# One bank for the four least loaded experts in w1's stage, capacities that fall by 16, and three buffers for w1's split pairs

## The chip, the cores and the metric

The kernel runs on one core of one Trainium2 chip. The metric is the device time of one execution in microseconds. The kernel before takes 1414.84 us as the median of three runs (1413.66 to 1415.68).

The engines that matter here are TensorE (PE, with weight loads shown apart as PEld), VectorE (DVE), ScalarE (ACT), GpSimd (POOL) and SyncE (SP), which issues most DMAs. Each engine works through its own queue in the order in which the kernel wrote it down.

## The reference

The output is a gated mix of an attention and a mixture of experts, both over the same 2048 rows of 448 numbers:

```python
x = A_x                                            # 1 x 2048 x 448
g = sigmoid((x * gate_w).sum(-1, keepdims=True))
a = attention(x, wqkv, wo)                         # 16 heads of 28, softmax over 2048 keys
logits = x @ w_gate                                # 8 experts
topk_idx = argsort(-logits)[:, :2]                 # each row goes to two of them
gates = softmax(the two logits)
for e in range(8):
    w = (gates * (topk_idx == e)).sum(-1, keepdims=True)
    b += w * (silu(x @ w1[e]) @ w2[e])             # w1: 448 x 1792, w2: 1792 x 448
out = g * a + (1 - g) * b
```

Only the rows that chose an expert are sent through it: 4096 pairs of row and expert, 512 per expert on average. The loads that this input gives, in falling order, are 561, 545, 514, 507, 501, 500, 497 and 471.

## The kernel before

**Precision.** Almost every product is made of three matmuls on a fast type: each operand is split into a high part (a rounded copy) and a low part (what the rounding lost), and high x high, high x low and low x high are added in PSUM. The splits are work for other engines. ACT makes the high parts, POOL (in the stage that matters here) the low ones.

**Stages.** First come the projections, the routing and its slot lists. Then, from 119 us to 885 us, come the eight experts (lines 868 to 992). The attention's scores and values fill the rest. Experts are handled in falling order of load, and expert number e of that order has `CAPS[e]` slots: `max(576 - 12*e, 512)`, so 576, 564, 552, 540, 528, 516, 512, 512. A row that finds no slot would be handled at the end by a slow loop (`spilled`); with this input none is.

**One expert** is done in two halves (`hf` 0 and 1) of 7 blocks of 128 hidden units each. Each half has a w1 stage and a w2 stage.

- *w1's stage* (line 904) makes a block of hidden units for all slots. A PSUM bank holds 512 columns, so the slots are cut into two chunks of `HC = CAPS[e] // 2` columns (288 down to 256), and each chunk takes 11 matmuls into one of two accumulators that alternate. ACT applies Silu (line 908) to each chunk as it comes out, and Copy (line 911) makes the high part `hh`. After the first chunk ACT also makes the high part of the w2 block that belongs to it (`split_w2_high`, line 767). After the second it makes, in some blocks, the high part of half a pair of w1 blocks that will be needed two blocks later (`split_w1_high`, line 730). POOL then makes, for each block and in this order, the low part of that w2 block (`w2l`, line 773), the low part of the half pair of w1 where there is one (`w1l`, line 736), and the low part of the block of hidden units before it (`hl`, line 782). The last `hl` of a half follows behind its last block. `hf32`, from which `hl` is made, has three buffers.
- *w2's stage* (line 956) adds up the outputs: four tiles of 128 slots, 21 matmuls of 448 columns each. The first tile already needs, in its 18 first matmuls, the low parts of blocks 1 to 6, and in the 20th and 21st `w2l` and `hl` of the last block. In the second half the next expert's rows are turned by TensorE between these matmuls (`turn_x`, line 755, after matmuls 6 and 15 in the first tile).
- Slots over 512 form a fifth, small tile. It is done by `last_slots` under a condition `tc.If(cnt > 512)` that every engine evaluates (line 934), after the third matmul of each w2 stage, for all experts with more than 512 slots of capacity: numbers 0 to 5.

**w1's split pairs.** Each w1 pair (256 hidden units) has a high and a low tile, two buffers of each; the first pair of all lies in another tile, `wv_r`, that the first stage had left. In a half with number 0, pairs are split in blocks 3 to 6 (counted from 1), and one pair whole at the start of w2's stage. In a half with number 1, they are split in blocks 2 to 5, and two pairs whole in w2's stage.

**The stream of maxima.** The attention needs the largest score of every row, which is 1024 tiles of 128x512 scores (line 118) that DVE reduces (lines 132 and 138). These are made in the experts' stages, in between: `STEPS` lists, for each expert, half and stage, after which matmul a step of this stream falls. A step makes 6 tiles in a PSUM area of six banks; where the number is positive, it makes a seventh in the accumulator that is just free, or, if 64 tiles are complete, spends that bank on turning their maxima round (`store_max`, line 154). A negative number makes 6 tiles and touches no accumulator. Steps come until all 1024 tiles are done, and only then may the first attention scores start (`first_scores`).

Of the kernel before, what the change touches and what calls it, by code (L numbers as in the profile page):

```python
# [9 lines left out]
F32R = mybir.dt.float32r  # L10
# [3 lines left out]
ALU = mybir.AluOpType  # L14
# [7 lines left out]


STEPS = [
# [8 lines left out]
]  # L33

S, D, H, DH, E, FF = 2048, 448, 16, 28, 8, 1792
NT = S // 128
NG = H // 4
CAP = 576
# [3 lines left out]
NTL = NMAIN // 128 + NSP  # L42
NS = NMAIN + NSP * 128

CAPS = [max(CAP - 12 * p, 512) for p in range(E)]
CTS = [[128] * 4 + [c - 512] * (c > 512) for c in CAPS]
NF = FF // 128
NH = NF // 2
# [12 lines left out]
def tile_gated_mha_moe(ctx: ExitStack, tc: tile.TileContext, x, xT, wv, wqk, wo, w1, w2, out):  # L61
    nc = tc.nc
# [131 lines left out]
    def step(bank):  # L194
        if bank and flush:
            store_max(*flush.pop(0), bank)
        elif bank:
            spare.append(bank)
        next(ms, None)
        spare.clear()  # L200
# [33 lines left out]
    def first_w():  # L234
        return pe.tile([128, 4, 512], F32, name="wv_r")
# [16 lines left out]
    with ExitStack() as pa:  # L252
# [113 lines left out]
        for t in range(NT):  # L366
# [11 lines left out]
            if 7 <= t < 15:  # L378
                b, c = divmod(t - 7, 2)
# [17 lines left out]
        def tmp(name, shape, dt=F32):  # L397
            return sb.tile(shape, dt, name=name)
# [5 lines left out]
        def routing():  # L404
# [49 lines left out]
            ahead = tmp("ahead", EE)  # L454
            nc.vector.tensor_tensor(ahead, bc(key.unsqueeze(1), EE), bc(key.unsqueeze(2), EE), op=ALU.is_gt)
            yield
            pos = tmp("pos", [128, E])
            nc.vector.tensor_reduce(pos, ahead, axis=AX.X, op=ALU.add)
            yield
            cap = tmp("cap", [128, E])  # L460
            nc.vector.tensor_scalar(cap, pos, -12.0, float(CAP), op0=ALU.mult, op1=ALU.add)
            nc.vector.tensor_scalar(cap, cap, 512.0, None, op0=ALU.max)
            yield
            nc.vector.tensor_tensor(key, cnt, cap, op=ALU.subtract)
# [7 lines left out]
            for e in range(E):  # L472
                nc.vector.tensor_tensor(sbase[:, e + 1:e + 2], sbase[:, e:e + 1], nsp[:, e:e + 1], op=ALU.add)
                if e % 4 == 3:
# [13 lines left out]
                                           op0=ALU.mult, op1=ALU.add)  # L488
# [147 lines left out]
        w1rs = [load_w1(0, c) for c in range(3)]  # L636
        for i, mt in enumerate((5, 2, 6)):
# [5 lines left out]
            if i == 0:  # L643
                nc.scalar.activation(warm[:, 1:2], warm[:, 0:1], AF.Silu)
                w1p = first_w().bitcast(F32R)
                w1t = {0: (w1rs.pop(0), w1p[:, :, 0:256], w1p[:, :, 256:512])}
# [59 lines left out]
    with ExitStack() as pb:  # L706
        sb1 = pb.enter_context(tc.tile_pool(name="pb_sb1", bufs=2, reuse_waits="tile"))
# [3 lines left out]
        NP = NF // 2  # L711
# [11 lines left out]
        def split_w1_high(p, half):  # L723
            if p >= E * NP:
                return
            if p not in w1t:
                w1t[p] = (w1rs.pop(0), sb1.tile([128, 4, 256], F32R, name="w1h"),
                          sb1.tile([128, 4, 256], F32R, name="w1l"))
            r, h, l = w1t[p]
            nc.scalar.activation(h[:, :, half], r[:, :, half], AF.Copy)  # L730

# [31 lines left out]
        WHOLE, HALVES = slice(0, 256), (slice(0, 128), slice(128, 256))  # L763
# [93 lines left out]
        NM = 11  # L857

        def behind(places, i):
            if i in places:  # L860
                step(other_accumulator())
            elif -i in places:
                step(None)

        for e in range(E):
            CT, HC = CTS[e], CAPS[e] // 2
            later = CTS[e + 1] if e + 1 < E else []
            if len(CT) == 5:
                cnt = nc.values_load(cnt_i[0:1, 0, e:e + 1], min_val=0, max_val=S)
# [6 lines left out]
            for hf in range(2):  # L876
                hs = []
                lag = None
                w1_steps, w2_steps = STEPS[e][hf]
                for f in range(NH):  # L880
                    ft = hf * NH + f
                    p = e * NP + ft // 2
                    i2 = e * NF + ft

                    w2_now = [i2] if e or hf else [i2 - 1, i2][f == 0:1 + (f == NH - 1)]

                    ahead = p + 1 if 2 <= ft < 6 or ft >= 8 and ft < 12 or e == 0 and ft < 2 else None
                    w1h, w1l = w1t[p][1:]
                    fs = HALVES[ft % 2]
                    if ft == 0:  # L890
                        flush_x()
                    mms = []
                    for j in range(3):
                        mms += [(w1h[:, j, fs], xeh[:, j]), (w1h[:, j, fs], xel[:, j]),
                                (w1l[:, j, fs], xeh[:, j])]
                    mms += [(w1h[:, 3, fs], xeh[:, 3]), (w1l[:, 3, fs], xeh[:, 3])]
                    hh = sb.tile([128, 512], F32R, name="hh", bufs=8)
                    hf32 = sb.tile([128, 512], F32, name="hf32", bufs=3)
                    ht = sb.tile([128, CAP - 512], F32, name="ht", bufs=8) if len(CT) == 5 else None
                    for c in range(2):  # L900
                        cs = slice(c * HC, (c + 1) * HC)
                        pu = accumulator()
                        for i, (a, b) in enumerate(mms):
                            nc.tensor.matmul(pu[:, 0:HC], a, b[:, cs], start=i == 0, stop=i == len(mms) - 1)  # L904
                            behind(w1_steps, 2 * NM * f + c * NM + i + 1)
                        nh = min(HC, 512 - c * HC)
                        hs_ = slice(c * HC, c * HC + nh)
                        nc.scalar.activation(hf32[:, hs_], pu[:, 0:nh], AF.Silu)  # L908
                        if ht and c == 1:
                            nc.scalar.activation(ht[:, 0:CT[4]], pu[:, nh:HC], AF.Silu)  # L910
                        nc.scalar.activation(hh[:, hs_], hf32[:, hs_], AF.Copy)
                        if c == 0:
                            for i in w2_now:
                                split_w2_high(i)
                        else:
                            if ahead:
                                split_w1_high(ahead, HALVES[ft % 2])
                    for i in w2_now:
                        split_w2_low(i)
                    if ahead:  # L920
                        split_w1_low(ahead, HALVES[ft % 2])
                    if lag:
                        hidden_low(lag)
                    hl = sb.tile([128, 512], F32R, name="hl", bufs=8)
                    lag = (hh, hf32, hl)
                    hs.append((hh, hl, ht))
# [10 lines left out]
                for n_k, k in enumerate((4, 0, 1, 2, 3)):  # L937
# [13 lines left out]
                    i = 0  # L951
# [34 lines left out]
                        nc.gpsimd.tensor_tensor(yo, yo, ysb[k], op=ALU.add)  # L986
                        nc.sync.dma_start(ys_d[r0:r0 + n], yo)

                    free = {0: ((e * NP + 4, 0),), 1: ((e * NP + NP, 0), (e * NP + NP + 1, 2))}[hf]
                    for p, at in free:  # L990
                        if n_k == at:
                            split_w1_high(p, WHOLE)
# [96 lines left out]
    qs, pos, ended = {0: q}, {}, {}  # L1089
# [123 lines left out]
```

## Time and profile before

| | before |
|---|---|
| median of three runs | 1414.84 us |
| the profiled execution's own time | 1413.67 us |
| its span in the profile | 1411.9 us |
| experts' stage (first matmul of line 904 to last of line 956) | 119.2 to 884.7 us |
| steps of the stream of maxima | 118 of seven tiles, 33 of six |

The profile is one execution. A busy TensorE says little here, since matmuls are pipelined and their shown durations overlap: what counts is the time from the start of one matmul to the start of the next. The timeline shows those starts. The table of stretches gives each engine's busy time in an expert.

### The profile page before, as it was taken

Reading aid. Unit: us, or ns where it says so; the run is one execution under the profiler, and the core shown is the slowest. Engines: PE = TensorE matmul, PEld = TensorE weight load, DVE = VectorE, ACT = ScalarE, POOL = GpSimd, SP = SyncE. Lnnn points to the kernel's source line nnn. Section 1 sums busy time; section 2 is a strip of 40 time slices with the busy share of each in tenths; the row PEclk is TensorE's granted clock in tenths of the full one; section 3 lists DMA queues with packets and bytes.
Section 4 is the critical chain, followed back from the end, with each engine's and each line's share of the span. In section 5 each row is a group of like instructions: output and inputs, shape, how many; then the busy total and the mean of one; then the engine's idle time right before and its main releaser. Section 6 shows DMA issues by size and latency. Waiting matters only on the chain. (4 is left out here: it accounts for less than half of the span.)

```text
span 1411.9 us, 28709 instructions
## 1 busy us (share of the span) xinstructions
PE 1399.9 (99%) x11028; PEld 931.1 (66%) x11028; DVE 799.5 (57%) x915; ACT 912.3 (65%) x1531; POOL 641.0 (45%) x682
## 2 busy tenths in 40 slices
PE   9999999999999999999999999999999999999998
PEld 8888888878878888888788887333333333333347
DVE  5736777777878888887888887013221212211136
ACT  5335355355445544654455434999999999999981
POOL 2124587487578666875777646121121122111120
PEclk9999999999999999999999999999999999999999
DMA  9887541343233233323432221111421332141113
GB/s 337 288 279 236 168 153 58 111 130 92 87 120 117 62 118 124 98 72 109 136 124 79 74 61 40 47 51 54 126 72 44 100 85 57 45 128 46 46 39 116
DMA packets 106685, 152.81 MB, mean 108 GB/s; under 512 B 17926, under 2 KB 77523, under 8 KB 106032
## 3 DMA queue, kind: packets, MB, share of 16 engines
q1 hardware_dynamic: 97392, 129.86, 29.2%
q0 software_dynamic: 9008, 20.83, 4.8%
q8 instruction: 89, 1.46, 0.4%
q14 instruction: 52, 0.43, 0.1%
q10 hardware_dynamic: 144, 0.23, 0.1%
HBM read 115.99 MB, written 38.02 MB: 109 GB/s over the span
## 5 line engine op out<-in xcount | busy, mean ns | idle before, releaser
L138 DVE TENSOR_REDUCE mp<-pm 128x3 f32<-128x1536 f32 (+2 forms) x304 | 515.7, 1738 | 32.3 <-PE pm L118 32.3
L1103 ACT ACTIVATE P<-ps 128x1536 f32<-128x1536 f32 x254 | 367.7, 1447 | 0.0
L1112 PE MATMUL po<-P,V 128*32 128x512 f32 x2032 | 270.6, 604 | 0.0
L904 PE MATMUL acc<-xeh,w1h 128*128 128x256 f32 (+6 forms) x880 | 252.8, 296 | 0.0
L904 PE MATMUL acc<-xeh,w1l 128*128 128x256 f32 (+6 forms) x880 | 247.0, 290 | 1.1 <-POOL w1l L736 1.1
L701 PEld LDWEIGHTS ps<-Q,Kh 29*128 29x128 f32 x2032 | 77.8, 183 | 212.6 <-ACT P L1102 212.3
L773 POOL TENSOR_TENSOR w2l<-w2r,w2h 128x448 fp32r<-128x448 f32 x112 | 129.5, 1157 | 156.1 <-ACT w2h L767 113.9
L1058 POOL DMA_DIRECT2D sum_d<-osb x64 | 32.3, 518 | 369.3 <-DVE osb L1116 369.3
L904 PE MATMUL acc<-xel,w1h 128*128 128x256 f32 (+6 forms) x660 | 189.7, 287 | 0.0
L701 PE MATMUL ps<-Q,Kh 29*128 29x512 f32 x2032 | 189.2, 443 | 0.0
L904 PEld LDWEIGHTS acc<-xeh,w1h 128*128 128x128 f32 x880 | 165.8, 188 | 25.4 <-issue 25.2
L956 PE MATMUL acc<-w2h,hh 128*128 128x448 f32 x448 | 171.2, 382 | 1.2 <-PEq L787 0.3
L904 PEld LDWEIGHTS acc<-xeh,w1l 128*128 128x128 f32 x880 | 166.0, 189 | 6.0 <-issue 2.9
L956 PE MATMUL acc<-w2h,hl 128*128 128x448 f32 x448 | 166.4, 371 | 0.2 <-POOL hl L782 0.2
L956 PE MATMUL acc<-w2l,hh 128*128 128x448 f32 x448 | 166.2, 371 | 0.0
L908 ACT ACTIVATE hf<-acc 128x256 f32<-128x256 f32 (+6 forms) x224 | 86.3, 385 | 113.6 <-PE acc L904 97.4
L1116 DVE COPY osb<-po 128x512 f32<-128x512 f32 x16 | 11.1, 692 | 261.3 <-PE po L1112 212.3
L1102 ACT ACTIVATE P<-ps 128x512 f32<-128x512 f32 x254 | 151.7, 597 | 1.4 <-ACT P L1103 0.5
L736 POOL TENSOR_TENSOR w1l<-w1r,w1h 128x512 fp32r<-128x512 f32 (+1 forms) x88 | 138.4, 1572 | 24.3 <-ACT w1h L730 20.3
L132 DVE TENSOR_REDUCE mp<-acc 128x1 f32<-128x512 f32 x118 | 81.6, 692 | 117.5 <-PE acc L118 110.4
L782 POOL TENSOR_TENSOR hl<-hf,hh 128x512 fp32r<-128x512 f32 x112 | 144.3, 1296 | 0.0
L904 PEld LDWEIGHTS acc<-xel,w1h 128*128 128x128 f32 x660 | 124.6, 189 | 1.3 <-issue 1.1
(214 smaller groups left out, 1987.1 us busy)
## 6 DMA issues: line engine op xcount, KB each, us to landing
w2r<-in_w_dram SPq DMA_DIRECT2D x112, 224.0 KB
w1r<-in_w_dram SPq DMA_DIRECT2D x56, 384.0 KB
ys_d<-zero_d SPq DMA_DIRECT2D x32, 224.0 KB
qkh_d<-hi SPq DMA_DIRECT2D x28, 256.0 KB
qkl_d<-lo SPq DMA_DIRECT2D x28, 256.0 KB
w1r<-in_w_dram SPq DMA_DIRECT2D x112, 64.0 KB
ys_d<-yo SPq DMA_DIRECT2D x32, 224.0 KB
v_d<-v_s SPq DMA_DIRECT2D x16, 256.0 KB
```

Source lines behind the costliest of these rows:

```text
L132: nc.vector.tensor_reduce(mp[:, o:o + 1], banks[0], axis=AX.X, op=ALU.max)
L138: nc.vector.tensor_reduce(mp[:, (o + lo) % 256:(o + lo) % 256 + hi - lo], pm[:, lo:hi], axis=AX.X, op=ALU.max)
L701: nc.tensor.matmul(banks[j], k[rw, ks], q[rw, c], start=i == 0, stop=i == 2)
L736: nc.gpsimd.tensor_tensor(l[:, :, half], r[:, :, half], h[:, :, half].bitcast(F32), op=ALU.subtract)
L773: nc.gpsimd.tensor_tensor(w2l, w2r, w2h.bitcast(F32), op=ALU.subtract)
L782: nc.gpsimd.tensor_tensor(hl, hf32, hh[:, 0:512].bitcast(F32), op=ALU.subtract)
L904: nc.tensor.matmul(pu[:, 0:HC], a, b[:, cs], start=i == 0, stop=i == len(mms) - 1)
L908: nc.scalar.activation(hf32[:, hs_], pu[:, 0:nh], AF.Silu)
L956: nc.tensor.matmul(py[:n, 0:D], a[:, cs], b, start=i == 0, stop=i == 3 * NH - 1)
L1102: nc.scalar.activation(P[:, 0], p1, AF.Exp, scale=SCALE)
L1103: nc.scalar.activation(P[:, 1:4], p3, AF.Exp, scale=SCALE)
L1112: nc.tensor.matmul(po[32 * j:32 * j + 32], v[:, kt % 8, 32 * j:32 * j + 32], P[:, j] if n > 1 else P[j], start=kt == 0, stop=kt == NT - 1)
```

## The change

- `CAPS` falls by 16 per expert: 576, 560, 544, 528, 512, 512, 512, 512. The routing's formula is changed with it.
- An expert with 512 slots (numbers 4 to 7) takes w1's stage in one chunk of 512 columns. A block is then 11 matmuls into one bank, one Silu and one Copy; `split_w2_high` and `split_w1_high` both follow after that one chunk. Experts 4 and 5 have no fifth tile any more.
- Every third pair of w1 lies in `wv_r`, so that there are three buffers.
- With the third buffer, the sixth pair is split whole in the w2 stage of half 0, and half 1 splits w1 pairs in blocks 4 and 5 alone.
- `STEPS` has new places. They hold 155 steps: 94 of seven tiles and 61 of six.

```diff
 STEPS = [
-    (([17, 50, 83, 116, 148], [13, 32, 51, 70]), ([7, 39, 72, -100, -124, 148], [-11, -25, 39, 59, 76])),
...
-    (([17, 50, 83, 116, 149], [18, 37, 56, 75]), ([17, 50, 83, 116, -149], [-11, -25, 39, 56, 75])),
-    (([17, 50, 83, 116, 148], [15, 34, 53, 72]), ([-12, 39, 72, 105, 138], [9, 28, 47, 67])),
+    (([-24, -48, 72, -100, -124, 148], [13, 32, 51, 70]), ([7, 39, 72, -100, -124, 148], [-11, -25, 39, 59, 76])),
+    (([17, 50, 83, 116, 148], [13, 32, 51, 70]), ([7, 39, -69, 94, -123, 148], [-11, -25, 39, 59, 76])),
+    (([17, 50, 83, 116, 149], [14, 33, 52, 71]), ([-9, -35, 61, -91, 116, 148], [-11, -25, 39, 59, 76])),
+    (([17, 50, 83, 116, 148], [13, 32, 51, 70]), ([-8, -34, 60, -90, 116, 148], [-11, -25, 39, 55, 74])),
+    (([8, 28, -45, 60, -77], [16, 35, 54, 73]), ([7, -24, 39, -56, 71], [-10, -24, 38, 55, 74])),
...
+    (([8, 28, -45, 60, -77], [16, 35, 54, 73]), ([7, -24, 39, -56, 71], [12, -31, 47, 67])),
 ]
...
-CAPS = [max(CAP - 12 * p, 512) for p in range(E)]
+CAPS = [max(CAP - 16 * p, 512) for p in range(E)]
...
             if p not in w1t:
-                w1t[p] = (w1rs.pop(0), sb1.tile([128, 4, 256], F32R, name="w1h"),
-                          sb1.tile([128, 4, 256], F32R, name="w1l"))
+                if p % 3:
+                    w1t[p] = (w1rs.pop(0), sb1.tile([128, 4, 256], F32R, name="w1h"),
+                              sb1.tile([128, 4, 256], F32R, name="w1l"))
+                else:
+                    w = first_w().bitcast(F32R)
+                    w1t[p] = (w1rs.pop(0), w[:, :, 0:256], w[:, :, 256:512])
...
-            CT, HC = CTS[e], CAPS[e] // 2
+            CT = CTS[e]
+
+            HC = CAPS[e] if CAPS[e] <= 512 else CAPS[e] // 2
+            NC = CAPS[e] // HC
...
-                    ahead = p + 1 if 2 <= ft < 6 or ft >= 8 and ft < 12 or e == 0 and ft < 2 else None
+                    ahead = p + 1 if 2 <= ft < 6 or ft in (10, 11) or e == 0 and ft < 2 else None
...
-                    for c in range(2):
+                    for c in range(NC):
...
-                            behind(w1_steps, 2 * NM * f + c * NM + i + 1)
+                            behind(w1_steps, NM * (NC * f + c) + i + 1)
...
-                        else:
-                            if ahead:
-                                split_w1_high(ahead, HALVES[ft % 2])
+                        if c == NC - 1 and ahead:
+                            split_w1_high(ahead, HALVES[ft % 2])
...
-                    free = {0: ((e * NP + 4, 0),), 1: ((e * NP + NP, 0), (e * NP + NP + 1, 2))}[hf]
+                    free = {0: ((e * NP + 4, 0), (e * NP + 5, 2)), 1: ((e * NP + NP, 0), (e * NP + NP + 1, 2))}[hf]
```

More of the change, by code (lines that the diff above doesn't have):

```diff
@@ L460, in routing @@
             cap = tmp("cap", [128, E])
-            nc.vector.tensor_scalar(cap, pos, -12.0, float(CAP), op0=ALU.mult, op1=ALU.add)
+            nc.vector.tensor_scalar(cap, pos, -16.0, float(CAP), op0=ALU.mult, op1=ALU.add)
             nc.vector.tensor_scalar(cap, cap, 512.0, None, op0=ALU.max)
```

7 rows, old and new, of the table STEPS are left out of this document.

## The prediction

> **What bounds the kernel now.** I read the page's busy times first, then the stretches expert by expert, then TensorE's waits, and then the timelines of PE, ACT and POOL in the seventh expert (number 6), which already has 512 slots.
>
> ```profile
> PE 1399.9 (99%) x11028; PEld 931.1 (66%) x11028; DVE 799.5 (57%) x915; ACT 912.3 (65%) x1531; POOL 641.0 (45%) x682
> ```
>
> ```profile
> core 0: us, PE busy (x) PEld busy (x) DVE busy (x) ACT busy (x) POOL busy (x), PEclk, DMA share, GB/s
> 515.12:608.40 93.28, 92.56 (x628) 76.91 (x627) 75.53 (x64) 46.30 (x118) 65.91 (x58) 1.00 0.33 103
> 608.40:701.12 92.72, 91.73 (x624) 75.97 (x623) 75.79 (x65) 45.83 (x115) 64.60 (x55) 1.00 0.33 105
> 701.12:792.87 91.75, 91.11 (x623) 76.05 (x622) 75.07 (x63) 45.32 (x101) 64.50 (x55) 1.00 0.33 101
> 792.87:884.74 91.87, 90.48 (x624) 75.15 (x622) 70.35 (x61) 43.91 (x97) 50.23 (x41) 1.00 0.17 51
> ```
>
> ```profile
> PE acc L904 <- POOL w1l L736: 1.1, 3, 0.7
> PE acc L956 <- POOL hl L782: 0.2, 1, 0.2
> ```
>
> The stretches are experts 4, 5, 6 and 7; the waits are us in total, times and longest, from 515 to 885 us. TensorE sets the time, at full clock, and waits for little. But the few waits for POOL fall in these experts, so I look at how close POOL is. POOL in the first half of expert 6, and TensorE at the half's first matmul, w2's first, and the 22nd of w2:
>
> ```profile
> 701.12 0.28 PE L904 MATMUL acc<-xeh,w1h 128*128 128x256 f32 x1
> 711.03 1.15 POOL L773 TENSOR_TENSOR w2l<-w2r,w2h 128x448 fp32r<-128x448 f32 x1 [1.11 <-ACT w2h L767]
> 712.42 1.29 POOL L736 TENSOR_TENSOR w1l<-w1r,w1h 128x512 fp32r<-128x512 f32 x1 [0.23 <-ACT w1h L730]
> 713.66 1.30 POOL L782 TENSOR_TENSOR hl<-hf,hh 128x512 fp32r<-128x512 f32 x1
> 714.90 1.17 POOL L773 TENSOR_TENSOR w2l<-w2r,w2h 128x448 fp32r<-128x448 f32 x1
> 716.00 1.31 POOL L736 TENSOR_TENSOR w1l<-w1r,w1h 128x512 fp32r<-128x512 f32 x1
> ...
> 724.30 0.39 PE L956 MATMUL acc<-w2h,hh 128*128 128x448 f32 x1
> 726.81 2.56 POOL L782 TENSOR_TENSOR hl<-hf,hh 128x512 fp32r<-128x512 f32 x2
> 728.18 0.47 PE L956 MATMUL acc<-w2h,hl 128*128 128x448 f32 x1 [0.24 <-POOL hl L782]
> 729.95 0.38 PE L956 MATMUL acc<-w2h,hh 128*128 128x448 f32 x1
> ```
>
> From 712.42 to 729.37 POOL has no gap. It finishes 28.25 us after the half began (729.37 - 701.12), TensorE starts the 22nd matmul of w2 at 28.83, and one matmul (728.18) has already waited. So POOL's 45% hides a stretch in which it is the bound within a fraction of a microsecond. That is what the change must be weighed against.
>
> **Prices.** TensorE's starts: twelve matmuls of 512 columns later in the projections, eleven of 256, nine of 448, and one step of the stream:
>
> ```profile
> 103.16 0.39 PE L603 MATMUL pq<-xh,wqk_h 128*128 128x512 f32 x1
> 105.88 0.39 PE L603 MATMUL pq<-xl,wqk_h 128*128 128x512 f32 x1
> 797.10 0.28 PE L904 MATMUL acc<-xeh,w1h 128*128 128x256 f32 x1
> 798.42 0.28 PE L904 MATMUL acc<-xeh,w1h 128*128 128x256 f32 x1
> 822.09 0.36 PE L956 MATMUL acc<-w2h,hh 128*128 128x448 f32 x1
> 823.92 0.36 PE L956 MATMUL acc<-w2h,hh 128*128 128x448 f32 x1
> 824.88 0.47 PE L956 MATMUL acc<-w2l,hh 128*128 128x448 f32 x1
> 825.18 0.36 PE L956 MATMUL acc<-w2h,hl 128*128 128x448 f32 x1
> ```
>
> That is 2.72/12 = 0.227, 1.32/11 = 0.120 and 1.83/9 = 0.203 us from start to start, and 0.083/192 = 0.43 ns per column. The step between 823.92 and 825.18 costs 1.26 - 2 x 0.203 = 0.86.
>
> ```profile
> L908 ACT ACTIVATE hf<-acc 128x256 f32<-128x256 f32 x56 | 21.6, 385 | 27.5 <-PE acc L904 23.1 <-POOL w2l L773 3.6
> L908 ACT ACTIVATE hf<-acc 128x288 f32<-128x288 f32 x14 | 5.8, 412 | 8.6 <-PE acc L904 8.6
> L911 ACT ACTIVATE hh<-hf 128x256 fp32r<-128x256 f32 x56 | 23.4, 418 | 1.8
> L911 ACT ACTIVATE hh<-hf 128x288 fp32r<-128x288 f32 x14 | 6.2, 445 | 0.4
> ```
>
> ```profile
> 768.92 0.36 PE L956 MATMUL acc<-w2h,hh 128*128 128x448 f32 x1
> 769.12 0.39 ACT L908 ACTIVATE hf<-acc 128x256 f32<-128x256 f32 x1 [0.80 <-PE acc L904]
> 769.54 0.42 ACT L911 ACTIVATE hh<-hf 128x256 fp32r<-128x256 f32 x1
> 760.73 0.42 ACT L911 ACTIVATE hh<-hf 128x256 fp32r<-128x256 f32 x1
> 761.05 0.56 ACT L767 ACTIVATE w2h<-w2r 128x448 fp32r<-128x448 f32 x1
> ```
>
> Silu starts 0.20 after TensorE goes on, Copy 0.42 after Silu, the w2 split 0.32 after Copy and lasts 0.56. Silu and Copy grow by 27/32 = 0.84 ns per column, so by 0.22 each for 512 (estimate from these rows).
>
> **The change, part by part.**
>
> *One chunk of 512.* A block's 22 matmuls at 0.120 (2.64) become 11 at 0.227 (2.50). Alone this is 14 x 0.14 = 2.0 us for an expert with 512 slots, more for number 4, whose chunks had 264 columns. The Trainium skill's page TensorE: Matmul & The Clock Gate (section "Wait — 56ns, not 53.3ns?") says that warm matmuls follow each other after N / 2.4 GHz + 2.5 ns, which speaks against this gain: by it two of 256 would take 218.3 ns and one of 512 215.8 ns, so only 0.4 us per expert. This trace does not agree at 256, where 120 is measured against its 109.
>
> *What the one chunk delays.* The w2 split and the w1 split, which ACT made after the first and second chunk, now both come after the whole block. From the end of a block, w2h is there after 0.20 + 0.64 + 0.54 + 0.56 = 1.94 us, and POOL starts 2.03 after it. Before, w2h came after the first chunk, mostly while the second ran.
>
> *Half 0 of experts 4 to 7.* The steps fall after matmuls 8, 28, 45, 60 and 77, so the seven blocks end at 3.36, 5.85, 9.21, 11.71, 15.07, 18.42 and 20.92 us, and w2 would start at 21.78. POOL's gapless run starts with block 3's w2l at 9.21 + 2.03 = 11.24, where before it was 711.03 - 701.12 = 9.91 plus a gap of 0.23. From there five w2l at 1.11, four w1l and six hl at 1.25 (starts in the rows above) are 18.05, so POOL ends at 29.3. TensorE without waits would come to matmul 22 of w2 at 21.78 + 21 x 0.203 + 0.86 = 26.9. It waits at three places: third matmul of blocks 5, 6 and 7 for w1l (0.6, 1.1, 0.3: block 5's w1l ends at 13.6, its third matmul could start at 13.0, and so on), and for the last two hl (0.8). That makes 2.8 us of waits, and matmul 22 starts at 29.7. The same reckoning for expert 6 before gives 28.25 for POOL's end, as measured, and 28.68 for matmul 22 where the trace has 28.83, so I add 0.15: 29.85, **1.0 us later than before**.
>
> *Half 1 of these experts.* Splits in blocks 4 and 5 only. Block 4 ends at 12.57, its w2l runs to 15.7, its w1l to 16.95; block 6 wants that at 16.4 and waits 0.6; block 7's w1l ends at 20.55 and is wanted 1.1 earlier. So 1.75 us of waits, w2 starts at 23.53. With the two turns of rows (0.46 each) that then stand ahead, hl is in time in experts 4 to 6. Expert 7 turns none and waits 0.8 more. Matmul 22 starts at 29.57 against 29.20 by the same reckoning before: **0.4 later**. Where the third buffer relieves POOL (two w1l fewer here), the latency of the one-chunk block takes its place.
>
> *The condition and the fifth tile.* Experts 4 and 5 lose both. Before, expert 5:
>
> ```profile
> 676.85 0.37 PE L956 MATMUL acc<-w2h,hl 128*128 128x448 f32 x1
> 677.37 0.44 PE L956 MATMUL acc<-w2h,hh 128*128 128x448 f32 x1
> 678.53 0.66 PE L755 MATMUL acc<-ident,xg 128*128 128x128 f32 x4 [0.32 <-ACTq L934]
> ```
>
> 0.3 us at the branch and the wait of the turned rows behind it. This, the wider chunks and the fifth tile's turn are why experts 4 and 5 take 93.28 and 92.72 and expert 6 91.75. After the change the three do the same work in the same order, so all get expert 6's time plus 1.0 plus 0.4: 93.15. Expert 7 gets 91.87 + 1.2 + 0.3 = 93.4 (its own half 0 stood at 28.6). Against before: -0.1, +0.4, +1.4, +1.5, so **+3.2**.
>
> *Steps.* With 155 steps instead of 151, four more at 0.86 = **+3.4**; all four lie in experts 0 to 3 (one each). DVE does the same 1024 tiles. Places that fall closer than before in experts 0, 2 and 3 (24 to 26 matmuls between two steps of six) may wait for DVE, at most 0.2 each: +0.8 at most, of which I take 0.5.
>
> *Capacities of experts 1 to 3.* 2, 4 and 6 columns fewer per chunk, 308 matmuls each: 12 x 308 x 0.43 ns = **-1.6**. Expert 4 receives no fifth tile's rows in expert 3's second half: -0.3 (estimate: four short transposes).
>
> *Third buffer, moved split.* The sixth pair's split (one high on ACT, one low on POOL, 2.4 us) moves into half 0's w2 stage, and with it the DMA of the pair three further on, which SP issues behind it. POOL has only row fetches and another such split there, and SP's queue behind it holds loads that are wanted one half later. I cost it at nothing; without that cover it would cost its 2.4 once per expert.
>
> **Sum:** 3.2 + 3.4 + 0.5 - 1.6 - 0.3 = +5.2 us. The profiled execution's own 1413.67 gives 1418.9; it lies 1.2 below the median of the three runs, and 1414.84 + 5.2 is 1420.0. I predict 1419.6.
>
> **The rivals.**
>
> 1. *Slower through POOL's lateness* (the forecast, 0.60).
> 2. *POOL keeps up* (faster, 0.16). This is the other side: one mechanism, POOL's run in the w1 stages of experts 4 to 7. If it ended 2.8 (half 0) and 1.75 us (half 1) earlier, TensorE would wait for nothing: 4 x (2.8 + 1.75) + 0.8 = 19 us less, 1400.6. For it speaks that POOL's total in half 1 has become smaller. Against it stand the rows: POOL had no gap from 712.42 on, and its three operations take the same time whatever TensorE does. If Silu and Copy of 512 took no longer than of 256, the run would start 0.44 earlier, 8 x 0.44 = 3.5 us less, 1416.1. The sign turns where it ends 0.65 us earlier per half (5.2/8). A page's rule bears on this rival in the other direction: the Trainium skill's Perfetto Trace Analysis (section "Optimizing Scalar/DVE Operations") says that where ScalarE isn't saturated but causes bubbles elsewhere, breaking up instructions may let work finish sooner. The change does the reverse, and ACT's 45.32 us of 91.75 show that it isn't saturated.
> 3. *Gains and waits cancel* (within 0.2%, 0.13). A 512-column matmul may follow after less than 0.227 us here, since only the projections show it. The lower bound by the rows is 512 x 0.43 ns = 0.220. Then block 3 ends 33 x 0.007 = 0.23 earlier, POOL's run starts so much earlier, and 8 x 0.23 = 1.9 us fall away; without the 0.5 for DVE it is 1417.2.
> 4. *DVE becomes a second bound* (slower still, 0.11). A step of seven before:
>
> ```profile
> 748.24 0.69 DVE L132 TENSOR_REDUCE mp<-acc 128x1 f32<-128x512 f32 x1 [1.06 <-PE acc L118]
> 748.85 3.41 DVE L138 TENSOR_REDUCE mp<-pm 128x3 f32<-128x1536 f32 x2
> ```
>
> DVE needs 4.0 us for it (748.24 to 752.26). In one-chunk experts some steps follow after 15 matmuls: 15 x 0.227 + 0.86 = 4.27 us. If each of the 40 steps in those stages waited 0.15, it would be 6 us more: 1425.6. Against it: steps of seven are followed by 17 matmuls or more.
>
> **How the numbers follow.** About 0.2% (2.8 us) is what a measurement here can tell from no change. Forecast and rival 4 are slower: 0.71. Rival 3 is the same: 0.13. Rival 2 is faster: 0.16. The range from 1411.5 to 1426 takes in rivals 3 and 4 and the upper part of rival 2, and leaves out most of the rest of 2. The forecast's own range is 1417.7 to 1423.
>
> **What would show it.** TensorE's waits for w1l and hl go from 1.3 us to some 12 or more, all in experts 4 to 7. Each of these has w2's start some 23.5 to 23.8 us after the half's, in spite of fewer matmuls. POOL's last hl ends near 29.3 us in half 0. Experts 4 to 7 take about 93 us each. Silu of 512 takes about 0.6 us. There are 155 steps. Wrong it would be if POOL's run begins earlier than 11.2, or if the 512-column matmuls follow after clearly less than 0.227.

## The result, and the profile after

The changed kernel takes 1422.3 us as the median of six runs (1421.41 to 1422.84), the kernel before 1414.75 us in six runs beside it (1413.66 to 1415.68). The ratio is 1.0053, with a 95% interval from 1.0042 to 1.0064: about 7.5 us slower. The profiled execution of after took 1422.84 us (span 1421.0), 9.2 us more than that of before.

Busy times of the page, after:

```profile
PE 1399.0 (98%) x10404; PEld 889.4 (63%) x10404; DVE 798.4 (56%) x900; ACT 888.3 (63%) x1377; POOL 637.7 (45%) x668
```

TensorE issues 624 matmuls fewer and ACT 154 instructions fewer, yet the span is 9.1 us longer. The stretches, one row per expert from 0 to 7. First before, where the prediction showed only experts 4 to 7:

```profile
core 0: us, PE busy (x) PEld busy (x) DVE busy (x) ACT busy (x) POOL busy (x), PEclk, DMA share, GB/s
119.18:222.14 102.96, 101.97 (x690) 84.05 (x688) 77.15 (x64) 49.23 (x124) 70.11 (x63) 1.00 0.55 169
222.14:322.21 100.07, 100.05 (x684) 82.48 (x683) 75.70 (x65) 48.19 (x122) 68.79 (x62) 1.00 0.33 100
322.21:421.44 99.23, 99.14 (x685) 81.25 (x683) 75.54 (x64) 48.07 (x122) 68.62 (x62) 1.00 0.32 99
421.44:515.12 93.68, 92.97 (x629) 77.42 (x627) 75.50 (x64) 46.42 (x118) 66.16 (x58) 1.00 0.34 107
```

The same view of after, all eight:

```profile
119.43:223.26 103.83, 103.09 (x692) 84.50 (x691) 78.68 (x63) 49.21 (x123) 70.06 (x62) 1.00 0.55 168
223.26:324.05 100.79, 100.63 (x689) 82.56 (x688) 78.09 (x66) 48.03 (x121) 68.62 (x61) 1.00 0.33 102
324.05:424.45 100.40, 99.82 (x689) 81.09 (x687) 77.83 (x64) 47.73 (x121) 68.46 (x61) 1.00 0.30 95
424.45:519.57 95.12, 93.00 (x628) 77.04 (x627) 78.49 (x66) 45.74 (x114) 64.69 (x54) 1.00 0.35 108
519.57:613.07 93.50, 90.61 (x467) 66.19 (x465) 72.96 (x59) 40.08 (x72) 64.50 (x54) 1.00 0.32 99
613.07:706.44 93.37, 90.76 (x466) 66.33 (x465) 73.04 (x60) 40.08 (x72) 64.49 (x54) 1.00 0.33 104
706.44:799.91 93.47, 90.71 (x467) 66.30 (x466) 73.18 (x61) 40.10 (x72) 64.49 (x54) 1.00 0.31 99
799.91:893.11 93.20, 90.09 (x465) 64.92 (x463) 67.61 (x57) 38.78 (x68) 50.19 (x40) 1.00 0.16 50
```

Experts 0 to 3 take 0.87, 0.72, 1.17 and 1.44 us longer than before, 4.2 in all. Experts 4 to 7 take 0.22, 0.65, 1.72 and 1.33 us longer, 3.9 in all. In the last four rows the second number says where: 93.4 us of the stretch hold 90.7 us of busy TensorE, where before 91.75 held 91.11. The engine that sets the time now stands idle for 2.6 us and more per expert. What it waits for, in the waits of after from 119 to 893 us (total, times, longest; `wv_r` is the third buffer of the w1 pairs):

```profile
PE acc L911 <- POOL w1l L740: 5.6, 10, 0.8
PE acc L911 <- POOL wv_r L740: 3.4, 6, 0.8
PE acc L962 <- POOL hl L786: 1.6, 5, 0.4
PE acc L154 <- ACT ysb L980: 1.1, 1, 1.1
PE acc L154 <- DVE mg L147: 1.1, 4, 0.4
```

The first three rows are waits for POOL: 10.6 us against 1.3 before. The last two were not among the waits of before. The timeline of after in the first half of expert 6, which begins at 706.44:

```profile
706.44 0.39 PE L911 MATMUL acc<-xeh,wv_r 128*128 128x512 f32 x1
...
717.79 1.15 POOL L777 TENSOR_TENSOR w2l<-w2r,w2h 128x448 fp32r<-128x448 f32 x1 [1.01 <-ACT w2h L771]
718.89 1.28 POOL L740 TENSOR_TENSOR w1l<-w1r,w1h 128x512 fp32r<-128x512 f32 x1
720.23 0.50 PE L911 MATMUL acc<-xeh,w1l 128*128 128x512 f32 x1 [0.36 <-POOL w1l L740]
722.49 1.28 POOL L740 TENSOR_TENSOR w1l<-w1r,w1h 128x512 fp32r<-128x512 f32 x1
723.82 0.50 PE L911 MATMUL acc<-xeh,w1l 128*128 128x512 f32 x1 [0.75 <-POOL w1l L740]
...
728.95 1.15 POOL L777 TENSOR_TENSOR w2l<-w2r,w2h 128x448 fp32r<-128x448 f32 x1 [0.33 <-ACT w2h L771]
...
730.36 0.47 PE L962 MATMUL acc<-w2h,hh 128*128 128x448 f32 x1
733.66 2.52 POOL L786 TENSOR_TENSOR hl<-hf,hh 128x512 fp32r<-128x512 f32 x2
736.23 0.47 PE L962 MATMUL acc<-w2h,hl 128*128 128x448 f32 x1 [0.36 <-POOL hl L786]
736.54 0.36 PE L962 MATMUL acc<-w2h,hh 128*128 128x448 f32 x1
```

Here POOL's run begins 11.35 us after the half (717.79). Its only gap is one of 0.33 us (before 728.95), in which POOL itself waits for ACT's `w2h`: a block that waited for POOL ends late, and so its own split comes late to POOL. Two third matmuls and one of w2's stage wait until POOL is done, the last `hl` ends at 736.18, which is 29.74 after the half began, and the 22nd matmul of w2 follows at 30.10. Before it was 28.83.

The listed waits are smaller than the time lost. From the matmul before the wait at 720.23 to the one after it (719.37 to 720.57) it is 1.20 us. The same stretch takes 0.57 in both_early, a run described below, where no such wait stands. So a listed wait of 0.36 cost 0.63, and in the same way the one of 0.75 cost 1.01.

The rest lies in the attention. Its values matmuls, before and then after (first and last start):

```profile
L1112 PE MATMUL po<-P,V x2032: 592/593/617, 889.4 to 1370.1; 128*32 128x512 f32 x185
```

```profile
L1118 PE MATMUL po<-P,V x2032: 592/593/618, 897.8 to 1380.1; 128*32 128x512 f32 x185
```

They take 482.3 us instead of 480.7. From the last of them to the end of the span it is 40.9 instead of 41.8 us, so 0.7 us net of this execution's 9.1 belong to a stage whose code the change doesn't touch.

### The profile page after: what moved, and what is told of

Same layout as the page of the kernel before. It is cut to its first block, busy times and chain, and to the rows that moved or that the text cites. A ratio compares the mean times of both kernels' runs of the same rounds, so it can differ in the third digit from the quotient of the medians.

```text
span 1421.0 us, 27227 instructions
## 1 busy us (share of the span) xinstructions
PE 1399.0 (98%) x10404; PEld 889.4 (63%) x10404; DVE 798.4 (56%) x900; ACT 888.3 (63%) x1377; POOL 637.7 (45%) x668
## 5 line engine op out<-in xcount | busy, mean ns | idle before, releaser
L138 DVE TENSOR_REDUCE mp<-pm 128x3 f32<-128x1536 f32 (+3 forms) x312 | 529.0, 1738 | 58.9 <-PE pm L118 58.9
L915 ACT ACTIVATE hf<-acc 128x512 f32<-128x512 f32 (+8 forms) x168 | 76.6, 456 | 156.3 <-PE acc L911 150.0
L911 PE MATMUL acc<-xeh,w1l 128*128 128x512 f32 (+4 forms) x440 | 144.2, 334 | 5.6 <-POOL w1l L740 5.6
L911 PE MATMUL acc<-xeh,w1h 128*128 128x512 f32 (+4 forms) x440 | 144.2, 333 | 0.0
L132 DVE TENSOR_REDUCE mp<-acc 128x1 f32<-128x512 f32 x95 | 65.7, 692 | 97.4 <-PE acc L118 89.0
L1072 DVE RECIPROCAL rs<-rs 128x128 f32<-128x128 f32 x64 | 60.6, 946 | 104.8 <-DMA rs<-sum_d 104.8
L118 PE MATMUL pm<-khg,qg 28*128 28x512 f32 x929 | 113.4, 449 | 0.7 <-issue 0.2
L911 PE MATMUL acc<-xeh,wv_r 128*128 128x512 f32 (+4 forms) x464 | 107.1, 329 | 3.4 <-POOL wv_r L740 3.4
L911 PE MATMUL acc<-xel,w1h 128*128 128x512 f32 (+4 forms) x330 | 109.0, 330 | 0.0
L740 POOL TENSOR_TENSOR w1l<-w1r,w1h 128x512 fp32r<-128x512 f32 (+1 forms) x53 | 91.6, 1727 | 38.2 <-ACT w1h L734 17.8
```

The lines of the kernel that those rows point to most:

```text
L118: nc.tensor.matmul(banks[n], qgs[g, qt // 4][rw, (qt % 4) * 128:(qt % 4 + 1) * 128], kh[g, kc][rw], start=True, stop=True)
L138: nc.vector.tensor_reduce(mp[:, (o + lo) % 256:(o + lo) % 256 + hi - lo], pm[:, lo:hi], axis=AX.X, op=ALU.max)
L740: nc.gpsimd.tensor_tensor(l[:, :, half], r[:, :, half], h[:, :, half].bitcast(F32), op=ALU.subtract)
```

## The experiments

There are two questions. Does the lost time come from *lateness* (the splits of ACT stand behind the whole block's Silu and Copy, so POOL starts late) or from the *amount* of POOL's work in a half that got shorter? And what costs 4.2 us in experts 0 to 3, which still work in two chunks? Times are medians; the kernel before took 1413.63 us beside the first four runs and 1414.69 beside the next three. "Experts end" is the start of the last matmul of w2's stage in the profile, a cleaner measure than the whole time, since the attention adds its own variation. It is 884.4 before and 892.7 after.

| run | time | ratio to before (95%) | experts end |
|---|---|---|---|
| two_chunks | 1408.57 | 0.9962 (0.9948 to 0.9977) | 880.2 |
| w2_early | 1410.90 | 0.9979 (0.9969 to 0.9988) | 882.1 |
| both_early | 1404.07 | 0.9931 (0.9914 to 0.9948) | 875.5 |
| one_bank | 1419.84 | 1.0046 (1.0029 to 1.0062) | 891.8 |
| no_hl | 1412.58 | 0.9985 (0.9975 to 0.9994) | 882.4 |
| third_buffer | 1413.54 | 0.9995 (0.9985 to 1.0004) | 883.0 |
| late_tails | 1403.82 | 0.9921 (0.9905 to 0.9938) | 873.8 |

**Everything but the single chunk and the new steps (two_chunks).** After, with all experts in two chunks and the `STEPS` of before:

```diff
...
-            HC = CAPS[e] if CAPS[e] <= 512 else CAPS[e] // 2
+            HC = CAPS[e] // 2
...
```

> The changed kernel, but all experts keep two chunks in w1's stage and the places of the steps are those of before (151 steps). Capacities falling by 16, the third buffer and the moved split stay. Theory (the one chunk makes POOL's work late and the four steps cost 0.86 each): without both, only gains are left. Narrower chunks in experts 1 to 3 -1.6 and in 4 and 5 -1.8, the condition and the fifth tile's turns in 3 to 5 -2.9, waits for w1l in the second halves -1.4: about 1407 us. Rival (the third buffer with its moved split, or the capacities, cost the time): 1418 or more.

It took 1408.57 us, 5.1 less than before: capacities, third buffer and moved split are a gain. The stretches of its experts 0 to 3 and 4 to 7:

```profile
119.40:514.00 394.60, 392.10 (x2679) 322.68 (x2678) 303.89 (x254) 190.75 (x479) 271.31 (x238) 1.00 0.39 120
514.00:880.53 366.53, 363.42 (x2492) 303.26 (x2490) 296.79 (x250) 179.21 (x396) 243.67 (x202) 1.00 0.30 91
```

This splits the loss. From here to after, experts 4 to 7 go from 366.5 to 373.5 us: the single chunk, with the places of steps that go with it, costs 7.0 us. Experts 0 to 3 go from 394.6 to 400.1: the new steps, four of them additional, cost 5.5. Against before, the narrower chunks and the missing turn of expert 4's fifth tile bring 1.3 us in experts 0 to 3 (395.9 to 394.6). In third_buffer, below, the same experts take 395.8, so the third buffer has hardly a part in that.

**The single chunk alone (one_bank).** Before, with one chunk in experts 6 and 7, whose capacity is 512 there too, and two steps more (153) in the rows of `STEPS` of experts 0, 1, 6 and 7. Two w1 buffers, old capacities:

```diff
...
-                    for c in range(2):
+                    for c in range(NC):
...
-                        else:
-                            if ahead:
-                                split_w1_high(ahead, HALVES[ft % 2])
+                        if c == NC - 1 and ahead:
+                            split_w1_high(ahead, HALVES[ft % 2])
```

> The kernel before with one part alone: experts 6 and 7, which have 512 slots already, take w1's stage in one chunk, with the changed kernel's places of steps there (and in experts 0 and 1, so that all tiles are made: 153 steps). Two buffers, no moved split, old capacities. Theory: the first halves of 6 and 7 get 1.3 and 1.5 us longer, the second ones 1.0 and 0.5 (reckoned with four splits in blocks 2 to 5), two more steps cost 1.7: +6.1, about 1420.9 us. Rival (one chunk of 512 is a gain for TensorE, 1.2 us per expert, and the loss comes from elsewhere): 1414.

It took 1419.84 us, 6.2 more. Experts 6 and 7 take 94.4 and 94.0 us, 4.8 us more than before together, and two steps at 0.86 are 1.7. So two experts in one chunk without the third buffer cost more than 2 us each, and the last `hl` ends up to 30.5 us after its half began. Waits from 119 to 892 us:

```profile
PE acc L906 <- POOL w1l L736: 5.3, 10, 0.8
PE acc L957 <- POOL hl L782: 0.7, 2, 0.4
```

**The order of ACT's work (w2_early, both_early).** After, where ACT makes the high parts *ahead* of the block's Silu and Copy. They don't depend on the block. First only w2's:

```diff
+                    if NC == 1:
+                        for i in w2_now:
+                            split_w2_high(i)
                     for c in range(NC):
...
-                        if c == 0:
+                        if c == 0 and NC == 2:
```

> As both_early, but only the w2 block's high part is made before the block's Silu; the w1 half pair stays behind Copy. Theory: POOL's run starts earlier, but its w1l still waits for the block; waits of 1.4 us per first half and 0.6 per second are left. 9.6 us less than the changed kernel: about 1412.7 us. Rival (amount of work): 1421 to 1423.

1410.90 us, 1.8 less than reckoned. The wait for `hl` is gone, the last `hl` of first halves ends 28.3 to 28.5 us after their start, and the waits for `w1l` and `wv_r` fall from 9.0 to 3.8 us (from 119 to 884 us), where 8.0 were reckoned to be left:

```profile
PE acc L914 <- POOL w1l L740: 2.4, 5, 0.6
PE acc L914 <- POOL wv_r L740: 1.4, 3, 0.5
```

Then both splits:

```diff
+                    if NC == 1:
+                        for i in w2_now:
+                            split_w2_high(i)
+                        if ahead:
+                            split_w1_high(ahead, HALVES[ft % 2])
                     for c in range(NC):
...
-                        if c == 0:
+                        if c == 0 and NC == 2:
...
-                        if c == NC - 1 and ahead:
+                        if c == NC - 1 and NC == 2 and ahead:
```

> The changed kernel, but in one-chunk blocks ACT makes the high parts of the w2 block and of the half pair of w1 before the block's Silu, not after its Copy. No work is added or taken away on any engine. Theory (lateness of POOL's run, because its inputs come after the whole block): reckoned as in the prediction with 0.232 us per matmul, no wait is left in the halves of experts 4 to 7; matmul 22 of w2 starts 2.6 us earlier in each first half, 1.6 in three second halves and 2.4 in the last, 17.7 us in sum: about 1404.6 us. Rival (POOL's amount of work is the bound, so order on ACT helps nothing): 1421 to 1423. Rival (steps or DVE): 1419 or more.

1404.07 us, 9.6 less than before, with the same instructions as after. The experts end 17.2 us earlier than in after (892.7 to 875.5). The first half of expert 6, which begins at 698.27:

```profile
698.27 0.39 PE L916 MATMUL acc<-xeh,wv_r 128*128 128x512 f32 x1
...
704.19 0.39 PE L916 MATMUL acc<-xeh,w1h 128*128 128x512 f32 x1
...
706.20 1.15 POOL L777 TENSOR_TENSOR w2l<-w2r,w2h 128x448 fp32r<-128x448 f32 x1
...
720.32 0.47 PE L967 MATMUL acc<-w2h,hh 128*128 128x448 f32 x1
721.78 2.52 POOL L786 TENSOR_TENSOR hl<-hf,hh 128x512 fp32r<-128x512 f32 x2
725.78 0.36 PE L967 MATMUL acc<-w2h,hh 128*128 128x448 f32 x1
```

Block 3's `w2l`, with which POOL's run began at 11.35 us, now starts at 7.93 (706.20), the last `hl` ends at 26.03, and no matmul waits for POOL any more. So this half shows what TensorE alone needs: w2 starts at 22.05 and its 22nd matmul at 27.51. In after it was 23.92 and 30.10. Lateness of POOL therefore costs 2.6 us in this half. In the second halves the 22nd matmul stands at 28.33 to 28.34 in experts 4 to 6, against 30.05 to 30.11 in after. Experts 4 to 7 together:

```profile
519.99:875.89 355.90, 355.11 (x1860) 265.26 (x1858) 286.78 (x233) 159.28 (x284) 243.59 (x202) 1.00 0.30 93
```

That is 355.9 us, 17.6 less than after and 10.6 less than two_chunks, while POOL is busy for as long as in after (243.59 us against 243.67, the sum of the four rows above) and TensorE idles for 0.8 us in all. One chunk, with its places of steps, is worth 10.6 us where its splits are early, and costs 7.0 where they are late. Two chunks with early splits were not tried. In two_chunks TensorE idles for 3.1 us in these experts (366.53 less 363.42), which leaves little for earlier splits to win there.

**The amount of POOL's work (no_hl).** After, without `hl` in experts 4 to 7 (`hh` stands in its place, so the low part of the hidden units is missing from their output):

```diff
+                    if NC == 1:
+                        hs.append((hh, hh, ht))
+                        continue
...
-                hidden_low(lag)
+                if NC == 2:
+                    hidden_low(lag)
```

> The changed kernel with POOL's hl left out in experts 4 to 7: w2's stage there uses hh a second time in place of hl, so TensorE does the same number of matmuls and the low part of the hidden units is missing from these experts' output. ACT's order stays as changed. Theory (both POOL's amount of work and the lateness of its inputs): the waits for hl go, but the first w1l still comes after the block; by the prediction's reckoning waits of 1.2 us per first half and 0.6 per second are left, 10.9 us less than the changed kernel: about 1411.4 us, and waits for w1l remain in the profile. Rival (POOL's amount of work alone): no waits are left, 1404 us as with both_early. Rival (lateness alone): 1421.

1412.58 us. Seven operations of 1.25 us leave POOL's queue in each half, and TensorE still waits (from 119 to 884 us):

```profile
PE acc L911 <- POOL w1l L740: 2.9, 8, 0.4
PE acc L911 <- POOL wv_r L740: 1.5, 4, 0.4
```

So neither explanation holds alone. Taking 8.75 us of work per half from POOL lets the experts end 10.3 us earlier than in after (882.4 against 892.7); letting it begin some 3.4 us earlier, with all its work, 17.2. A delayed start and a full queue add up to the finish that TensorE waits for, and the start is the cheaper one to mend.

**The third buffer alone (third_buffer).** Before, with three buffers and the moved split:

```diff
...
-                    ahead = p + 1 if 2 <= ft < 6 or ft >= 8 and ft < 12 or e == 0 and ft < 2 else None
+                    ahead = p + 1 if 2 <= ft < 6 or ft in (10, 11) or e == 0 and ft < 2 else None
...
-                    free = {0: ((e * NP + 4, 0),), 1: ((e * NP + NP, 0), (e * NP + NP + 1, 2))}[hf]
+                    free = {0: ((e * NP + 4, 0), (e * NP + 5, 2)), 1: ((e * NP + NP, 0), (e * NP + NP + 1, 2))}[hf]
```

> The kernel before with one part alone: three buffers for w1's split pairs, the sixth pair's split moved into the first half's w2 stage. Theory (the moved split is hidden and takes two w1l off POOL in each second half): the waits for w1l in the second halves of experts 5 to 7 go, 0.3, 0.35 and 0.9 us: about 1412.3 us, 0.1% faster. Rival (the moved split stands in a queue's way, in the prediction's price up to 2.4 us per expert): slower, up to 1432.

1413.54 us, 1.2 less than before, which can't be told from no change. The waits for `w1l` of before (1.1 us) are gone, and the experts end 1.4 us earlier. The moved split costs nothing where it went.

**Expert 3's stall (late_tails).** The waits of after list one for ACT's `ysb`. TensorE in expert 3's first half, then ACT and POOL around it:

```profile
460.13 0.37 PE L962 MATMUL acc<-w2h,hl 128*128 128x448 f32 x1
461.62 0.28 PE L154 MATMUL acc<-ident,mg 128*16 128x128 f32 x1 [1.12 <-ACT ysb L980]
```

```profile
453.03 1.04 POOL L209 DMA_INDIRECT xg<-in_x_dram,idx_i  x1 [0.16 <-issue]
454.37 0.97 POOL L209 DMA_INDIRECT xg<-in_x_dram,idx_i  x1 [0.30 <-issue]
...
459.07 0.26 ACT L169 ACTIVATE xg<-xg 128x64 f32<-128x64 f32 x1 [4.93 <-issue]
460.88 0.26 ACT L169 ACTIVATE xg<-xg 128x64 f32<-128x64 f32 x1 [1.55 <-DMA xg<-in_x_dram,idx_i]
461.04 0.53 ACT L980 ACTIVATE ysb<-acc 128x448 f32<-128x448 f32 x1
```

ACT doubles the tails of the next expert's fetched rows (line 169). The first two fetches were issued at 453.03 and 454.37, ACT begins the first of them at 459.07, and the second at 460.88; the copy that empties the accumulator (`ysb`, 461.04) stands behind them. (The profile names the fetch as the cause of the second wait alone; in both_early it names it for both.) The new step after matmul 51 wants that accumulator to turn its maxima and waits 1.1 us for it. Before, ACT waited for these rows too (`ysb` at 458.13), but there the step followed after matmul 57. Both_early has the same stall, 1.7 us there, and w2_early 0.6. This run is both_early with the tails moved behind the half's last tile:

```diff
-                            for j in {0: (), 1: (0, 1)}.get(n_k, (n_k,)):
+                            for j in range(5) if n_k == 4 else ():
```

> As both_early, and ACT doubles the tails of the next expert's fetched rows (line 169) after the first half's w2 stage instead of during it. The changed kernel's profile shows a wait of 1.1 us of a step in expert 3 for ACT's ysb, and ACT waiting just before it for rows on their way. Theory: in the changed kernel the step that now stands after matmul 51 needs a bank that ACT empties only after its wait for these rows; moved behind, that wait goes (1.8 us from start to start in both_early) and 1402.2 us is left, expert 3's first half some 44.5 us instead of 46.3. Rival (that wait has another cause, or the tails are then late for the turn of rows): 1404 or more.

The stall is gone. The same step waits for nothing, and `ysb` is no longer in the list of TensorE's waits:

```profile
460.55 0.27 PE L154 MATMUL acc<-ident,mg 128*16 128x128 f32 x1
```

Expert 3's first half takes 44.61 us instead of 46.25, and the experts end 1.7 us earlier. The time, 1403.82 us, can't be told from both_early's 1404.07 and is not the 1402.2 that was expected: this execution's values matmuls took 482.8 us where both_early's took 480.8 between the first and the last. The kernel before was slower too beside this run. Against it late_tails gains 10.9 us, both_early 9.6, and the intervals of the two ratios overlap.

**The attention's variation (after_again, late_tails_again).** One more look at each of the two, unchanged, to see whether the longer values stage belongs to the program or to the execution.

> The changed kernel unaltered, one more profile. In its first profile the attention's values stage took 1.6 us longer than before from its first to its last matmul (487.4 - 5.0 against 485.8 - 5.0), in a few single passes. If that belongs to the program, it is there again at the same passes; if to the execution, it is elsewhere or gone. The experts' stage should take 773.3 us as in the first profile, to 0.3.

> late_tails unaltered, one more profile. Its attention's values stage took 2.1 us longer than both_early's, in a few single passes, which hid the 1.7 us that its experts' stage was shorter. If that belongs to the execution, the passes are elsewhere or gone, and the time of this execution is up to 2 us below 1403.8; if to the program, they are there again.

The times were 1424.01 and 1403.92 us, and the values matmuls took 482.7 and 482.1. The experts' stage of after_again took 773.3 us, as expected. Some passes of the values stage, which take 1.90 us as a rule, take 2.05 to 2.5. Numbers 67, 194 and 195 (counted from 0) were long in all four looks at these two kernels; others came and went. Before and both_early show none or one such pass.

That would speak for the program, but the other runs speak against it. Third_buffer and no_hl, two other programs, have the same three long passes. What the runs share is the chip that they ran on. The four profiles from one chip (two_chunks, w2_early, both_early, one_bank) have values stages of 480.8 to 480.9 us. The three from a second chip (no_hl, third_buffer, late_tails) have 481.8 to 483.1, the two from a third 482.7 and 482.1. The kernel before, beside them, took 1413.63, 1414.69 and 1415.33 us. On which chips the first profiles of before and after were taken is not known, and none of the other programs was profiled both on the first chip and on another. So the chip fits better than the program, but the cause stays open. It is worth 0 to 2 us of values time, of which the end of the kernel gave back 0.9 in after's first profile.

## Why the prediction was right, and where its sizes were off

The direction was as predicted, and so was the mechanism in experts 4 to 7: slower through POOL's lateness. But more than half of the experts' loss, 4.2 of 8.1 us, lies in experts 0 to 3, where 2.0 of 5.2 was forecast. The range held, but the likeliest value was 2.7 us low, just inside the forecast's own range (1422.3 against 1423); a later execution of the same kernel, with 1424.01, is outside it, so there is some luck in that. TensorE's listed waits for POOL came to 10.6 us, not "some 12 or more". By the prediction's steps:

- **Half 0 of experts 4 to 7.** POOL's start 11.24 (measured 11.35 in expert 6), its last `hl` 29.3 (29.74 in expert 6; 29.74 to 29.84 in all), matmul 22 at 29.85 (30.10 to 30.20). The run was taken as gapless; 0.33 of the 0.44 us that the last `hl` came later is the gap before 728.95. Waits were put at 2.8 us and are 2.6 by the comparison with both_early. What was low is TensorE's own work: I had 26.9 us to matmul 22 (and 0.15 added by comparison with before), both_early shows 27.51. The first two blocks and one step take 5.92 us (698.27 to 704.19), so (5.92 - 0.86)/22 = 0.230 per 512-column matmul instead of 0.227: 0.23 us over 77 matmuls. The other 0.34 lie in w2's stage, 5.46 us from its first matmul to the 22nd instead of 5.12: 0.10 behind the step that stands before it, and 0.24 in its own step, whose six tiles start that much after the seventh (724.00 and 723.76). In half 0 this hardly mattered, because POOL sets the end there.
- **Half 1.** Waits 1.75 predicted; 30.05 to 30.11 against 28.33 to 28.34 is 1.7 to 1.8. w2 was to start at 23.53 and does so at 23.9 to 24.0 (24.45 in expert 7, which was not looked into), in part through the longer 512-column matmuls. The sum of the four experts is +3.9 where +3.2 was predicted.
- **The gain of the wider matmul.** 2.0 us per expert was predicted. It is there, and more than eaten up by the waits: expert 6's first half, less its five steps of 0.86, takes 245 ns for two matmuls of 256 in two_chunks (w2 starts at 23.17) and 230 for one of 512 in both_early (22.05). That is 15 ns for each of 154 pairs, 2.2 us per expert. By the rule of the Trainium skill's TensorE: Matmul & The Clock Gate (section "Wait — 56ns, not 53.3ns?"), N / 2.4 GHz + 2.5 ns, the estimate is 218.3 ns for two matmuls of 256 columns and 215.8 for one of 512. The trace agrees with neither figure.
- **Silu of 512 columns** was estimated at 0.6 us; the groups by form of after have 599 ns, and 631 ns for Copy against 0.64:

```profile
L915 ACT ACTIVATE hf<-acc 128x512 f32<-128x512 f32 x56 | 33.5, 599 | 89.2 <-PE acc L911 86.5 <-PEq L791 2.7
L918 ACT ACTIVATE hh<-hf 128x512 fp32r<-128x512 f32 x56 | 35.4, 631 | 1.8
```

- **Experts 0 to 3** hold the term that was off in size: +2.0 predicted (3.4 for steps, 0.5 for DVE, less 1.6 and 0.3), +4.2 measured. Two_chunks shows that the narrower chunks and the fifth tile brought 1.3 rather than 1.9, and that the steps cost 5.5 rather than 3.9. Four steps at 0.86 are 3.4 of this. Most of the rest is DVE, which was put at 0.5. In a step of seven tiles the seventh and the six start together when the six banks are free. In experts 0 to 3 of after the six start 0.07 to 0.27 us later in 13 steps, 2.2 us in all; in two_chunks in 6 steps, 0.8 us. One of them, in expert 2:

```profile
386.88 3.42 DVE L138 TENSOR_REDUCE mp<-pm 128x4 f32<-128x2048 f32 x2 [0.71 <-PE pm L118]
390.09 0.50 PE L118 MATMUL acc<-khg,qg 28*128 28x512 f32 x1
390.35 0.73 PE L118 MATMUL pm<-khg,qg 28*128 28x512 f32 x6
```

  DVE reads the six banks until 390.30 (386.88 + 3.42), and the next six tiles start at 390.35. TensorE counts as busy there with the seventh tile, so no wait is listed. The listed waits for `mg`, which is DVE's work too, rose in these experts from 0.3 to 0.9 us. Together DVE cost 2.0 us more than in two_chunks. Expert 3's stall, which was not priced, cost 1.1: I had not asked which accumulator the moved step takes and who empties it. Against this, a wait of 1.1 us that two_chunks has in expert 0 (a step that waits for ACT's `ht`) is gone with the new places. 3.4 + 2.0 + 1.1 - 1.1 is 5.4 of the 5.5. For the stall there is a run, late_tails; DVE's part is read from the traces and was not tried by itself.
- **Third buffer and moved split: nothing.** Confirmed by third_buffer.
- **The attention** was not in the sum. It took 0.7 us more in the profile of after; its cause is open.

The rivals: *POOL keeps up* fell, with 10.6 us of waits listed for POOL. Its price was right in kind: it gave 1400.6, and both_early, in which POOL does keep up, measured 1404.07. *Gains and waits cancel* needed 0.220 per matmul and fell with 0.230. *DVE as a second bound* fell where it was looked for: in experts 4 to 7, where it would have cost 6 us, the late six tiles add up to 1.3 us in after and 0.9 in two_chunks. In experts 0 to 3 it was there, with the 2.0 us above.

The page's rule that the prediction set beside rival 2, the Trainium skill's Perfetto Trace Analysis (section "Optimizing Scalar/DVE Operations"), pointed the right way for this change: two chunks finish 7.0 us sooner than the one chunk of after. But both_early gains without breaking up anything. In this trace the bubble came from the place of the splits in ACT's queue, and that could be changed alone.

## What to carry to other kernels

Merging two pieces of work into one saves fixed cost on the engine that is the bound, but everything that was issued between the two pieces moves to the end; look for what stands there and doesn't depend on them, and issue it first. Judge a helper engine by the gapless run in one stage and by when that run may start, not by its share of the span: POOL was busy for 45% of the span in the kernel that waits for it and in the one that doesn't. When an added piece of work borrows a buffer, price not only its length but also what stands in the queue of the engine that empties the buffer. When steps move closer together, compare starts and not listed waits alone: a late start while the engine still counts as busy is in no list.

## What the runs showed of the hardware that was not expected

- A 512-column matmul follows after 0.230 us in the experts' stage (both_early) and after 0.227 in the projections (before).
- A listed wait of TensorE is less than what it costs: 0.36 listed cost 0.63 us from start to start, 0.75 listed cost 1.01 (after against both_early, first half of expert 6).
- ACT's work on rows that POOL's indirect DMA fetched began 6.0 and 6.5 us after the fetch was issued (453.03 to 459.07, 454.37 to 460.88), with ACT idle before; in both_early it was 6.1 and 7.1 us. With such waits at the head of ACT's queue TensorE waited 0.6 (w2_early) to 1.7 us (both_early) for an accumulator.
- The attention's passes of 1.90 us are now and then 2.1 to 2.5 us long, some at the same places in different programs, with up to 2 us in all. The profiles from one chip had 480.8 to 480.9 us of values time and those from two others 481.8 to 483.1; the cause is open.
